# One kernel, two k halves on two DMA queues: new order of the first loads, masked S on GpSimd, k sketch split by row halves

## The chip, the cores and the metric

The kernel runs on one core of a Trainium2 chip. The metric is the device time of one execution in microseconds (us); of several executions the median is given. The engines are named as the profile names them: PE is TensorE (PEld its weight loads), DVE is VectorE, ACT is ScalarE, POOL is GpSimd, SP is SyncE. SP and ACT issue the DMAs.

## The reference, cut to what matters

A polynomial linear attention feeds one feed-forward layer. All inputs are float32; there are 4 batches and 4 heads, 1088 positions, head size 32, and sketches S1 and S2 of 8 rows each.

```python
def phi(x):
    a = np.einsum('rd,bhsd->bhsr', S1, x)
    b = np.einsum('rd,bhsd->bhsr', S2, x)
    return np.einsum('bhsi,bhsj->bhsij', a, b).reshape(*x.shape[:-1], r * r)
q_p, k_p = phi(q), phi(k)
kv = np.einsum('bhsf,bhsd->bhfd', k_p, v)
z = np.sum(k_p, axis=2)
attn = np.einsum('bhsf,bhfd->bhsd', q_p, kv) / (np.einsum('bhsf,bhf->bhs', q_p, z)[..., None] + 1e-06)
x = attn as 4352 tokens x 128
h = x @ w_in                    # 128 -> 2048
out = (h - np.tanh(h)) @ w_out  # 2048 -> 128
```

## The kernel before, in words

The attention is computed batch by batch, the feed-forward in ten groups of tokens (192 to 512 columns each). The first group of tokens (384 columns) needs only the first 12 of the 34 q blocks of batch 0, and a special path (`q_heads`) makes them early. Until that group's x is there, PE has little to do, and runs matmuls on zeros (`f` of 256 and `F` of 512 columns) to stay busy. From then on PE works through the matmuls of the feed-forward (`h` and `o`) with the attention of the other batches between them.

Every operation is added to a program with its inputs and outputs (`P.add`), under a name. The order on each engine is not worked out when the kernel is built: it is written out in `TABLE`, a list of tokens such as `66t:0` (operation 66, on TensorE, buffer choice 0). `plan` reads the table, and `sync` puts semaphore waits where an operation needs one of another engine. Each engine then works strictly in its order. An operation marked `lock` also waits for the last locked operation of the other engine of the pair DVE and POOL. Large loads carry an extra wait, so that at most `CAP` bytes are in flight.

The start of batch 0, which the change touches, goes so:

- Loads (line 465). `load_k(0)` asks for k of batch 0 in two halves by columns, `lk0.0` and `lk0.1`, 272 KB each, on SP's queue; `sin1`, S2's load (16 KB), is on SP's queue too. `sin0` is S1's load, on ACT's queue. SP's order is `lk0.0`, `lk0.1`, `sin1`, then q, then v.
- Masks. POOL builds an identity matrix (lines 434, 435); DVE reduces it to `mask4` (line 439), `mask2` (442) and `maskh` (445).
- k transposes (line 560) on DVE, four of them: `kT0.0.0` and `kT0.1.0` of the first half (288 and 256 elements in each partition), `kT0.0.1` and `kT0.1.1` of the second.
- S. `stt` (line 524, DVE) transposes S1 and S2, which came by `sin0` and `sin1`; `wab` (line 527) multiplies it by `mask2`.
- Sketch. `ksk0.0` and `ksk0.1` (line 580, PE) are 16 calls in all, 32 matmuls in the profile: a call for each of four column groups and two row halves, for either half of k. `kab0.0` and `kab0.1` (line 591, DVE) transpose the result into `abk`, row half by row half.
- Outer products (line 646): `w0.0` on POOL, `w0.1` on DVE, `w0.2` on POOL, one after the other by the lock. `kvmm0.0` to `kvmm0.2` (line 661, PE) multiply them with v.
- The first q blocks: `qsk0.0`, `abc0.0`, `m0.0`, `den0.0` (line 712), `rd0.0` (714), `aq0.0` (POOL, 715), `qph0.0` and `qph0.1` (DVE, 722), `qpTh0.0` and `qpTh0.1` (728). In the same stretch stand `kvh` (689), `kve` (690), and, for the other 22 blocks, `m0.3` (774), `den0.3` (777) and `rd0.3` (780). POOL also copies S for batch 1, `wqc1` (534).
- `num0.0` and `num0.1` (line 735, PE), then the copies `x0.0.0` and `x0.0.1` (line 359), then the first feed-forward matmul `h0.0` (line 920).

Of the kernel before, what the change touches and what calls it, by code (L numbers as in the profile page):

```python
# [31 lines left out]
38s 125t:0 117v:0 251a:1 232g 253a:2 254t:0 43s 233g 256t:1 126v:1 280t:0 39s 255a:3 281t 282t 127v 258t:2 257a:4 234g
260t:0 119v 40s 128t:0 259a:5 262t:1 14g 283t 41s 129a:1 264t:2 261a:6 235v 284t 130t 263a:7 266t:0 36s 285t 265a:8
286t 131v:0 37s 133v:3 268t:1 287t 267a:9 288t 270t:2 269a:10 242t:0 134v:4 243t 271a:11 272t:1 289t 274t:2 273a:12
120t:0 45s 158v:0 275a:13 46s 132v 159v 276t:1 102s 244t 121a 135v:0 245t 44s 122a 278t:2 136t:0 277a:14 103s 137t
246a 138t 247v 48s 160t:1 142v 139a:1 105s 279a:15 303t:0 290t 104s 140t 161v:0 304a:16 305t:1 291t 162v 100s 307t:0
141a:1 309t:2 306a:17 143t:0 168g:1 308a:18 99s 310a:19 311t:0 292t 313t:1 144v:0 312a:20 293t 47s 315t:2 294t 314a:21
295t 101s 317t:0 316a:22 296t 319t:1 318a:23 297t 145g:0 321t:2 163t:0 320a:24 298v:0 323t:0 322a:25 57g 325t:1 146v:0
299s 164a:0 327t:2 324a:26 165t 335t:0 147v:0 326a:27 98s 336t 329t:0 166v:1 328a:0 148v:0 331t:1 300s 337t 330a:28
167v 333t:2 149g:1 177v 338t 301s 332a:29 339t 340t 341t 334a:1 358t:0 302s 360t:1 362t:2 359a:2 178t:0 151g:2 361a:30  # L40
150v:1 363a:31 364t:0 342t 366t:1 343t 365a:3 179v:1 368t:2 344t 367a:4 345t 153g:0 370t:0 369a:32 346t 372t:1 371a:33
374t:2 347t 152v 373a:5 348t 376t:0 375a:6 378t:1 180g:1 349t 377a:7 350t 154v 351t 380t:2 379a:8 352t 382t:0 381a:9
384t:1 353v:1 155t:0 383a:10 181v:1 354s 385a:11 355s 390t:0 356s 386t:0 157v 156a 391t 392t 357s 388t:1 393t 387a:12
170v:2 413t:2 394t 389a:13 415t:0 414a:14 395t 417t:1 182v:1 396t 212v 416a:15 397t 183g:1 398t 419t:2 418a:16 421t:0
184g:1 399t 400t 420a:17 401t 193v:0 423t:1 402t 422a:18 403t 404t 194v 425t:2 424a:19 405t 169g:3 406t 427t:0 426a:20
407t 429t:1 428a:21 431t:2 408v:2 195t:0 430a:22 185v:0 409s 58g 186g:2 432a:23 433t:0 410s 435t:1 196v:1 437t:2
434a:24 411s 171t:2 197v 436a:25 172t 412s 203g:4 198t:0 438a:26 173t 199a:1 439t:0 200t 174v:0 441t:1 440a:27 445t:0
11g 201v:0 443t:2 187v 188g:0 446t 442a:0 468t:0 447t 444a:28 470t:1 202v 175t 469a:29 472t:2 448t 59g 176v:2 471a:1
204g:0 474t:0 213t:0 189v 473a:2 475a:30 476t:1 449t 214v:0 205g:1 478t:2 477a:31 480t:0 450t 479a:3 451t 482t:1
481a:4 452t 453t 454t 483a:32 215v:0 484t:0 486t:2 216v:0 488t:1 485a:33 190t:0 217v:0 487a:5 218v:0 489a:6 219g:1  # L50
490t:0 191v 492t:1 455t 491a:7 494t:2 456t 192v 221g:2 493a:8 496t:0 457t 495a:9 458t 220v:1 498t:1 459t 497a:10 460t
523t:2 223g:0 499a:11 222v 461t 462t 524a:12 526t:0 529t:1 463v:0 206t:0 527a:13 207t 525v 530a:14 464s 532t:2 528v
500t:0 465s 531v 501t 533a:15 224v 535t:0 466s 502t 538t:1 536a:16 503t 467s 534v 504t 539a:17 537v 541t:2 505t 544t:0
540v 542a:18 506t 547t:1 545a:19 507t 543v 508t 548a:20 550t:2 546v 509t 510t 551a:21 549v 553t:0 511t 556t:1 552v
554a:22 512t 559t:2 557a:23 513t 555v 514t 560a:24 562t:0 558v 515t 516t 563a:25 561v 565t:1 517t 568t:2 564v 566a:26
208t 518v:1 569a:27 598t:0 567v 519s 571t:0 570v 599a:0 601t:1 572t 520s 604t:2 602a:28 600v 573t 521s 574t 605a:29
607t:0 603v 575t 522s 576t 608a:1 606v 610t:1 577t 613t:2 609v 611a:2 578t 579t 209v:1 616t:0 614a:30 580t 612v 581t
617a:31 582t 615v 619t:1 583t 618v 622t:2 620a:3 584t 625t:0 623a:4 585t 621v 586t 626a:32 587t 624v 628t:1 210t 627v
631t:2 629a:33 588t 211v:3 634t:0 632a:5 225t:0 630v 635a:6 589v:2 633v 590s 636v 637t:1 591s 646t:0 227a 226v 640t:0
592s 643t:2 638a:7 647t 648t 593s 641a:8 669t:0 639v 670t 594s 644a:9 673t:1 642v 649t 674t 671a:5 595s 645v 677t:2  # L60
650t 596s 651t 652t 675a:6 672v 678t 597s 653t 654t 655t 656t 679a:7 681t:0 676v 682t 657t 658t 659t 683a:8 680v
685t:1 686t 660t 661t 687a:9 684v 689t:2 690t 662t 663t 691a:10 701t:1 688v 693t:0 694t 702t 703t 695a:11 692v 697t:1
704t 698t 664v:0 705t 728t:2 699a:12 706t 696v 729t 665s 707t 708t 666s 730a:13 709t 700v 710t 732t:0 733t 667s 711t
712t 734a:14 731v 668s 736t:1 737t 713t 714t 738a:0 740t:2 735v 741t 715t 716t 742a:15 717t 739v 718t 744t:0 745t
760t:0 743v 748t:1 746a:1 749t 761t 762t 719v:1 752t:2 750a:16 753t 763t 747v 720s 764t 765t 721s 754a:2 766t 751v
756t:0 757t 722s 767t 768t 783t:1 758a:3 755v 769t 723s 770t 771t 784t 724s 772t 786t:2 787t 785a:4 759v 773t 725s
774t 788a:5 789t:1 790t 775t 726s 792t:0 793t 791a:6 795t:2 776t 727s 796t 794a:7 798t:1 799t 777t 797a:8 807t:1
801t:0 808t 802t 778v:2 800a:9 809t 804t:2 805t 810t 811t 803a:10 812t 813t 814t 781s 815t 816t 806a:11 817t 818t 819t
820t 779a 821t 782s 822t 823t 824t 780a 825v:0 827a 826s 829a 828s
# [260 lines left out]
def bass_polysketch_attn__then__act_tanh_shrink_kernel(  # L330
# [177 lines left out]

    load_s(0, S1, "scalar")
    load_k(0)  # L510
# [8 lines left out]
    for b in range(1, B - 1):  # L519
# [3 lines left out]

    P.add(_v(64), lambda e, n: e.transpose(
        stt.ap.rearrange("p x d -> p (x d)"), sin.ap.rearrange("p x d -> p (x d)")),
        r=[sin], w=[stt], name="stt")
    P.add(_v(32), lambda e, n: e.tensor_tensor(
        out=wab.ap.rearrange("p (x e i) -> p x e i", e=2, x=2),
        in0=stt.ap.rearrange("p x (r i) -> p x r i", i=8)[:, :, 0:2, :],
        in1=mask2.ap[:, None, :, None].to_broadcast([128, 2, 2, 8]), op=ALU.mult),  # L530
        r=[stt, mask2], w=[wab], name="wab", lock=True)
    for i, (w, z) in enumerate(zip(wqc, wqs)):
        P.add(_g(8), lambda e, n, z=z: e.memset(z[:, 24:32], 0.0), w=[w], name=f"wqz{i}")
        P.add(_g(16), lambda e, n, w=w: e.tensor_copy(
            w.ap.rearrange("p (x i) -> p x i", i=8), stt.ap.rearrange("p x (r i) -> p x r i", i=8)[:, :, 0, :]),
            r=[stt], w=[w], name=f"wqc{i}", lock=True)
    P.add(_gt(64), lambda e, n: e.tensor_tensor(
        out=wqdc.ap.rearrange("p h (x i) -> p h x i", i=8),
        in0=stt.ap.rearrange("p x (r i) -> p x r i", i=8)[:, None, :, 0, :].to_broadcast([128, H, 2, 8]),
        in1=maskh.ap[:, :, None, None].to_broadcast([128, H, 2, 8]), op=ALU.mult),  # L540
        r=[stt, maskh], w=[wqdc], name="wqd", lock=True)
    P.add(_gt(128), lambda e, n: e.tensor_tensor(
        out=s2r.ap.rearrange("p (h d) -> p h d", h=H),
        in0=sin.ap[:, 1, None, :].to_broadcast([128, H, 32]),
        in1=mask4.ap[:, :, None].to_broadcast([128, H, 32]), op=ALU.mult),
        r=[sin, mask4], w=[s2r], name="s2r", lock=True)

# [291 lines left out]
    def q_front(b, s0, s1):  # L839
        abc = _Val(abc_p)  # L840
        q_sketch(b, s0, s1, abc)
        return abc, q_divide(b, s0, s1, abc)

    def attention():
        k_transposes(0)
        k_sketch(0)
        gram(0)
        for p in range(3):
# [190 lines left out]
```

## Time and profile before

| what | value |
|---|---|
| time, median of 3 runs | 104.55 us (104.22 to 104.70) |
| the profiled execution's own time | 104.33 us |
| its span | 102.2 us |
| busy: PE, DVE, ACT, POOL | 94.9, 79.1, 79.7, 35.6 us |
| first feed-forward matmul (line 920) | starts at 17.33 us |
| feed-forward groups, tanh on ACT (line 924) | 40.5 + 16.8 + 16.6 us busy |
| DMA | 11.37 MB, 111 GB/s over the span |

The span runs from the first to the last instruction that the profile shows; the 2.1 us by which the execution's own time is longer lie around it. Times of instructions count from the start of the span. An engine's busy time says how long its instructions ran; what an engine waited for stands behind an arrow. The chain of waits is followed back from the last instruction, at each step to what released it.

### The profile page before, as it was taken

The numbers are of one execution on the slowest core, as the hardware profiler recorded it, in microseconds if no ns is written. First come the engines' busy times: TensorE is split into PE (matmuls) and PEld (weight loads), VectorE is DVE, ScalarE is ACT, GpSimd is POOL, SyncE is SP. The second block draws the span as 40 slices with busy tenths as digits, with TensorE's granted clock in tenths as the row PEclk, the third lists the DMA queues.
The fourth block names the chain that finished last, engine by engine and source line by source line (L and its number), as shares of the span: only waits on it lengthen the run. The fifth ranks groups of instructions, "written<-read, shape, count | busy, mean of one in ns | idle before, by whom it ended". The sixth has DMA issues, their size and how long they took to land.

```text
span 102.2 us, 3037 instructions
## 1 busy us (share of the span) xinstructions
PE 94.9 (93%) x1252; PEld 48.3 (47%) x1261; DVE 79.1 (77%) x146; ACT 79.7 (78%) x157; POOL 35.6 (35%) x53
## 2 busy tenths in 40 slices
PE   5998979999999999999999999999999999999950
PEld 2243546466645455555535343444453444444740
DVE  2678699989848896976697788687898789999420
ACT  4001395997689996999899798999988999999930
POOL 4066829900053991299892970000000000000000
PEclk9999999999999999999999999999999999999999
DMA  2987998999988811303100003305000410601555
GB/s 49 293 272 186 339 275 237 278 313 335 302 251 274 189 20 23 47 7 61 17 0 6 0 0 57 52 0 91 12 0 15 74 21 0 103 0 22 79 77 75
DMA packets 25917, 11.37 MB, mean 111 GB/s; under 512 B 19120, under 2 KB 23600, under 8 KB 25904
## 3 DMA queue, kind: packets, MB, share of 16 engines
q1 hardware_dynamic: 24288, 10.98, 42.2%
q10 hardware_dynamic: 1616, 0.20, 1.3%
q8 instruction: 10, 0.16, 0.7%
q14 instruction: 3, 0.02, 0.1%
HBM read 8.95 MB, written 2.23 MB: 109 GB/s over the span
## 4 chain that ended last, share of the span: by engine, by line
PE 64%; DVE 12%; POOL 9%; ACT 4%; issue 3%; DMA 3%; SPq 1%; DVEq 0%
PE psb L941 23%; PE psb L920 22%; POOL qp L800 4%; POOL w L646 4%; PE psb L661 4%; PE psb L580 3%; DMA sin<-in_S_dram 3%; PE psb L816 3%; DVE th L929 2%; DVE ot L950 2%; PE psb L945 2%; PE psb L757 2%; ACT wi_f L924 2%; PE psb L735 2%; DVE qp L722 1%
## 5 line engine op out<-in xcount | busy, mean ns | idle before, releaser
L920 PE MATMUL psb<-xT,wi 128*128 128x512 bf16 (+3 forms) x152 | 46.2, 347 | 0.2 <-issue 0.2
L924 ACT ACTIVATE th<-psb 128x512 bf16<-128x512 f32 (+3 forms) x77 | 40.5, 594 | 3.1 <-PE psb L920 1.8
L941 PE MATMUL psb<-th,wo 128*128 128x512 bf16 (+3 forms) x89 | 26.2, 343 | 0.5 <-DVE ot L950 0.2
L920 PEld LDWEIGHTS psb<-xT,wi 128*128 128x128 bf16 x160 | 14.8, 97 | 22.9 <-ACT th L924 4.4
L800 POOL TENSOR_TENSOR qp<-ap,abc 128x768 f32<-128x768 f32 x11 | 16.4, 1513 | 3.8 <-DVE ap L782 3.4
L924 ACT ACTIVATE wi_f<-psb 128x512 bf16<-128x512 f32 (+3 forms) x31 | 16.8, 612 | 0.5 <-PE psb L920 0.3
L924 ACT ACTIVATE wo_f<-psb 128x512 bf16<-128x512 f32 (+2 forms) x28 | 16.6, 626 | 0.7 <-PE psb L661 0.4
L929 DVE TENSOR_TENSOR th<-psb,th 128x320 bf16<-128x320 f32 (+2 forms) x24 | 13.2, 562 | 2.4 <-ACT th L924 1.6
L646 POOL TENSOR_TENSOR w<-abk 128x768 f32<-128x768 f32 x7 | 10.6, 1516 | 9.4 <-DVE abk L591 8.4
L941 PEld LDWEIGHTS psb<-th,wo 128*128 128x128 bf16 x90 | 8.6, 99 | 5.7 <-issue 0.5
L805 DVE STREAM_TRANSPOSE qpT<-qp 128x768 f32<-128x768 f32 x11 | 10.4, 955 | 0.6 <-POOL qp L800 0.6
L941 PE MATMUL psb<-wo_f,wo 128*128 128x512 bf16 (+1 forms) x32 | 10.4, 362 | 0.4 <-DVE th L929 0.4
L941 PE MATMUL psb<-wi_f,wo 128*128 128x512 bf16 (+2 forms) x38 | 10.3, 344 | 0.1
L430 PE MATMUL psb<-zz 128*128 128x512 bf16 x24 | 8.0, 456 | 1.1 <-DVE zz L428 1.1
L950 DVE STREAM_TRANSPOSE ot<-psb 128x512 f32<-128x512 f32 (+3 forms) x10 | 6.3, 628 | 3.3 <-PE psb L941 2.1
L929 DVE TENSOR_TENSOR wi_f<-psb,wi_f 128x192 bf16<-128x192 f32 (+1 forms) x12 | 6.1, 510 | 1.6 <-ACT wi_f L924 0.9
L929 DVE TENSOR_TENSOR wo_f<-psb,wo_f 128x320 bf16<-128x320 f32 (+2 forms) x12 | 6.8, 576 | 0.4 <-ACT wo_f L924 0.2
L560 DVE STREAM_TRANSPOSE kT<-kL 128x576 f32<-128x576 f32 (+3 forms) x10 | 5.8, 610 | 1.3 <-DMA kL<-in_k_dram 1.3
L762 DVE STREAM_TRANSPOSE abc<-psb 128x1152 f32<-128x1152 f32 (+1 forms) x4 | 5.1, 1273 | 1.9 <-PE psb L757 1.9
L816 PE MATMUL psb<-qpT,kvb 32*32 32x288 f32 (+1 forms) x256 | 6.1, 392 | 0.0
L661 PE MATMUL psb<-w,vL 128*32 128x64 f32 x288 | 5.4, 221 | 0.1
L661 PEld LDWEIGHTS psb<-w,vL 128*32 128x32 f32 x288 | 4.4, 110 | 1.8 <-issue 1.3
(89 smaller groups left out, 98.0 us busy)
## 6 DMA issues: line engine op xcount, KB each, us to landing
vL<-in_v_dram SPq DMA_DIRECT2D x16, 144.0 KB, 4.1
kL<-in_k_dram SPq DMA_DIRECT2D x8, 272.0 KB, 4.5
qL<-in_q_dram SPq DMA_DIRECT2D x6, 272.0 KB, 4.3
wi_f<-in_moe_w_in_dram SPq DMA_DIRECT2D x4, 256.0 KB, 5.4
wo_f<-in_moe_w_out_dram SPq DMA_DIRECT2D x4, 256.0 KB, 4.3
out_dram<-ot SPq DMA_DIRECT2D x14, 64.0 KB, 2.0
out_dram<-ot SPq DMA_DIRECT2D x8, 48.0 KB, 3.2
qL<-in_q_dram SPq DMA_DIRECT2D x2, 176.0 KB, 3.3
```

What stands on the lines that cost most here:

```text
L430: "F": lambda e, n: e.matmul(bank(3), zz.ap[:, 0:128], zz.ap[:, None, 128:384].to_broadcast([128, 2, 256]), start=True, stop=True)}, zop)
L560: P.add(_v(nb * 32 * (r1 - r0)), lambda e, n, e_=e_, nb=nb, r0=r0, r1=r1: e.transpose(kTv[b][r0].ap.rearrange("p (j u t r) -> p r j u t", ...
L646: P.add({**_v(768), **_gt(768)}, lambda e, n: e.tensor_tensor(out=wv.ap.rearrange("p (x i j) -> p x i j", i=8, j=8), in0=abh(0)[:, :, :, N ...
L661: i = e.matmul(pv[b].ap[h * 32:(h + 1) * 32, 0:64], vL[b][:, h, blk * 32:(blk + 1) * 32], wvs[b, p].ap[:, (bi * 4 + h) * 64:(bi * 4 + h + ...
L800: P.add({**_v(cn * 256), **_gt(cn * 256)}, lambda e, n, qp=qp, c0=c0, cn=cn: e.tensor_tensor(out=qp.ap[:, 0:cn * 256].rearrange("p (x i j) ...
L805: P.add(_v(cn * 256), lambda e, n, qp=qp, o0=o0, cn=cn: e.transpose(qt.ap[:, o0 * 256:(o0 + cn) * 256], qp.ap[:, 0:cn * 256]), r=[qp], w=[ ...
L816: i = e.matmul(psa4[h * 32:(h + 1) * 32, g, 0:nb * 32], kvb.ap[g * 32:(g + 1) * 32, x, h * 32:(h + 1) * 32], qq[g * 32:(g + 1) * 32, 0:nb, ...
L920: P.add(_mm(n_), lambda e, n, jb=jb, hv=hv: e.matmul(hv.ap[:, jb % m * 512:jb % m * 512 + n_], wi[jb // 4].ap[:, (jb % 4) * 128:(jb % 4 + ...
L924: act = P.add(_a(n_ * m), lambda e, n, hv=hv, th=th: e.activation(out=th.ap.rearrange("p (u x) -> p u x", u=m)[:, :, 0:n_], in_=hv.ap.rear ...
L929: P.add(_vp(gc * m), lambda e, n, hv=hv, th=th: e.tensor_tensor(out=th.ap.rearrange("p (u x) -> p u x", u=m)[:, :, 0:gc], in0=hv.ap.rearra ...
L941: fn = lambda e, n, x=x, st=st, sp_=sp_: e.matmul(ov.ap[:, 0:n_], wo[x // 4].ap[:, x % 4, :], ths[x][0].ap[:, ths[x][1] * 512:ths[x][1] * ...
L950: P.add(_vp(n_), lambda e, n: e.transpose(ot.ap[:, 0:n_], ov.ap[:, 0:n_]), r=[ov], w=[ot], name=f"ot{gi}")
```

## The change

The code changes in four places.

1. `load_k(0)` now comes ahead of `load_s(0, S1, "scalar")`, and the second half of k, `lk0.1`, is issued on ACT's queue. On ACT's queue the order is `lk0.1`, then `sin0`; on SP's it is `lk0.0`, then `sin1`, then q and v.
2. The block that makes the weights out of S moves into a function `s_weights()`, called after the k transposes, and `stt` must follow `kT0.0.1`.
3. `wab` may run on POOL, and the new table puts it there.
4. `ksk0.1` is split into two operations by row half, `ksk0.1` (first row half) and `ksk0.2` (second), so that `kab0.0` waits only for the first of them.

```diff
     def load_k(b):
         src = k[b].rearrange("h (t c) d -> (h t) (c d)", c=NC)
         for r in range(2):
-            load(kL[b][:, r * 544:(r + 1) * 544], src[:, r * 544:(r + 1) * 544], [kvals[b][r]], 128 * 544 * 4, 128, name=f"lk{b}.{r}")
+            load(kL[b][:, r * 544:(r + 1) * 544], src[:, r * 544:(r + 1) * 544], [kvals[b][r]], 128 * 544 * 4, 128, eng="scalar" if (b, r) == (0, 1) else "sync", occ=650.0 if (b, r) == (0, 1) else 415.0, name=f"lk{b}.{r}")
             if b == 0 and r == 0:
                 load_s(1, S2, "sync")
...
+    load_k(0)
     load_s(0, S1, "scalar")
-    load_k(0)
     load_q(0, 0)
...
+    def s_weights():
+        P.add(_v(64), lambda e, n: e.transpose(
+            stt.ap.rearrange("p x d -> p (x d)"), sin.ap.rearrange("p x d -> p (x d)")),
+            r=[sin], w=[stt], name="stt", after=[x for x in P.ops if x.name == "kT0.0.1"])
+        P.add({**_v(32), **_gt(32)}, lambda e, n: e.tensor_tensor(
+            out=wab.ap.rearrange("p (x e i) -> p x e i", e=2, x=2),
...
-        def sk(e, n, m0=0, ms=1):
+        def sk(e, n, m0=0, ms=1, rhs=(0, 1)):
             for g in range(4):
-                for rh in range(2):
+                for rh in rhs:
...
         if b == 0:
-            for r in range(2):
-                P.add(_pe(317, 245.0), lambda e, n, r=r: sk(e, n, r, 2), r=[kTv[b][r], wab], w=pk, mode="64x32", name=f"ksk{b}.{r}")
+            P.add(_pe(317, 245.0), lambda e, n: sk(e, n, 0, 2), r=[kTv[b][0], wab], w=pk, mode="64x32", name=f"ksk{b}.0")
+            for rh in range(2):
+                P.add(_pe(159, 245.0), lambda e, n, rh=rh: sk(e, n, 1, 2, (rh,)), r=[kTv[b][1], wab], w=[pk[rh]], mode="64x32", name=f"ksk{b}.{1 + rh}")
```

The table is written anew. Put into names, its orders differ from those of before in these places up to the first feed-forward matmul:

- DVE: `mask2` stood between `mask4` and `kT0.0.0`, and now stands between `kT0.1.0` and `kT0.0.1`; `wab` is gone; `den0.0` and `kvh` change places, and so do `kve` and `rd0.3`; `x0.0.0` is gone (it is on ACT, ahead of `x0.0.1`).
- POOL: `wab` stands right behind the identity matrix, ahead of `wqd`; four small fills and copies (`qpad0`, `qpad1`, `wqc0`, `wqdz`) stand later than they did.
- PE: one more `f` ahead of `ksk0.0`; of the fillers between the sketch and `num0.0` some are moved, and the `f` between `kvmm0.1` and `kvmm0.2` is gone. The numbers of `f` and `F` in the whole program change by one `f` less.
- SP: `lk0.1` is gone; `lq0.1.1` and `lq0.0.0` change places.

Behind the first feed-forward matmul the new table swaps neighbours in a few dozen places on PE (an `o` matmul and an `h` matmul, mostly), gives some banks and buffers other numbers, moves `x0.3.0` from ACT to DVE, `w1.2` ahead of `kT2.0.0` and `wo0` ahead of `qp0.6`, and changes the order in which SP asks for the later q and v pieces.

More of the change, by code (lines that the diff above doesn't have):

```diff
@@ L32 @@
[L32 to L36, printed above, removed]
@@ new lines @@
+8g 77v:1 7g F F F 85t:0 35s 75v 78g:2 111t:0 86v:0 79t:1 112v:1 80t 87g:0 81t 9g 88v:0 113g:1 34s 229a 82v 89v:0 59g
+90g:0 114v:1 108a:0 28s F F F F 109t 230a 91v:0 237t:0 95v:1 49s 231a 238t 115v:1 83v 240t:1 31s 232a 92v:0 116g:1
+239a 96v:1 F 241t 117g:2 32s 110v:0 93t:2 242a 97t:1 33s 94a 124v:0 98a f F F 249t:0 125v 233g 251t:1 42s 253t:2
+250a:0 38s 126t:0 118v:0 119g:0 252a:1 254a:2 255t:0 43s 281t:0 127v:1 257t:1 256a:3 282t 40s 283t 128v 259t:2 234g
+258a:4 261t:0 120v 41s 129t:0 260a:5 263t:1 61g 235g 284t 39s 130a:1 265t:2 262a:6 285t 131t 14g 264a:7 286t 236v
@@ new lines @@
+449t 473t:2 472a:28 205g:0 475t:0 190v 214t:0 474a:29 476a:3 477t:1 479t:2 215v:0 206g:1 450t 478a:30 451t 481t:0
+480a:31 483t:1 452t 482a:4 453t 485t:2 454t 484a:5 216v:0 455t 487t:0 486a:32 217v:0 489t:1 191t:0 488a:33 218v:0
+490a:6 219v:0 220g:1 491t:0 192v 493t:1 495t:2 492a:7 456t 457t 193v 222g:2 494a:8 497t:0 458t 496a:9 459t 221v:1
+499t:1 460t 498a:10 524t:2 461t 224g:0 500a:11 223v 462t 463t 525a:12 527t:0 530t:1 464v:0 207t:0 528a:13 208t 526v
+531a:14 465s 533t:2 529v 501t:0 466s 532v 502t 534a:15 225v 536t:0 467s 503t 539t:1 537a:16 504t 468s 535v 505t
@@ new lines @@
+540a:17 538v 542t:2 506t 545t:0 541v 543a:18 507t 548t:1 546a:19 508t 544v 509t 549a:20 551t:2 547v 510t 511t 552a:21
+550v 554t:0 512t 557t:1 553v 555a:22 513t 560t:2 558a:23 514t 556v 515t 561a:24 563t:0 559v 516t 517t 564a:25 562v
+566t:1 518t 569t:2 565v 567a:26 209t 519v:1 570a:27 599t:0 568v 520s 572t:0 571v 600a:0 602t:1 573t 521s 605t:2 603a:1
+601v 574t 522s 575t 606a:2 608t:0 604v 576t 523s 577t 609a:28 607v 611t:1 578t 614t:2 610v 612a:29 579t 580t 210v:1
+617t:0 615a:3 581t 613v 582t 618a:30 583t 616v 620t:1 584t 619v 623t:2 621a:31 585t 626t:0 624a:4 586t 622v 587t
@@ new lines @@
+627a:5 588t 625v 629t:1 211t 628v 632t:2 630a:32 589t 212v:3 635t:0 633a:33 226t:0 631v 636a:6 634v 590v:2 638t:1 637v
+591s 647t:0 228a 227v 641t:0 592s 644t:2 639a:7 648t 593s 649t 642a:8 670t:0 640v 671t 594s 645a:9 674t:1 643v 650t
+595s 675t 672a:5 646v 678t:2 651t 596s 652t 679t 676a:6 597s 673v 653t 654t 655t 656t 598s 657t 680a:7 682t:0 677v
+683t 658t 659t 660t 684a:8 681v 686t:1 687t 661t 662t 688a:9 685v 690t:2 691t 663t 664t 692a:10 694t:0 689v 702t:1
+703t 695t 704t 693v 698t:1 696a:11 705t 699t 665v:0 706t 707t 700a:12 729t:2 697v 730t 666s 708t 709t 667s 731a:13
@@ L70 @@
+817t 807a:11 818t 819t 820t 821t 783s 822t 780a 823t 824t 825t 781a 826v:0 828a 827s 830a 829s
 """
@@ L522, in bass_polysketch_attn__then__act_tanh_shrink_kernel @@
         load_v(b)
[L524 to L546, printed above, removed]
     xvals = []
@@ L563, in k_transposes @@
                     r=kvals[b][r0:r1], w=kTv[b][r0:r1], name=f"kT{b}.{e_}.{r0}")
+    def s_weights():
[4 more added lines that the diff above has]
+            out=wab.ap.rearrange("p (x e i) -> p x e i", e=2, x=2),
+            in0=stt.ap.rearrange("p x (r i) -> p x r i", i=8)[:, :, 0:2, :],
+            in1=mask2.ap[:, None, :, None].to_broadcast([128, 2, 2, 8]), op=ALU.mult),
+            r=[stt, mask2], w=[wab], name="wab", lock=True)
+        for i, (w, z) in enumerate(zip(wqc, wqs)):
+            P.add(_g(8), lambda e, n, z=z: e.memset(z[:, 24:32], 0.0), w=[w], name=f"wqz{i}")
+            P.add(_g(16), lambda e, n, w=w: e.tensor_copy(
+                w.ap.rearrange("p (x i) -> p x i", i=8), stt.ap.rearrange("p x (r i) -> p x r i", i=8)[:, :, 0, :]),
+                r=[stt], w=[w], name=f"wqc{i}", lock=True)
+        P.add(_gt(64), lambda e, n: e.tensor_tensor(
+            out=wqdc.ap.rearrange("p h (x i) -> p h x i", i=8),
+            in0=stt.ap.rearrange("p x (r i) -> p x r i", i=8)[:, None, :, 0, :].to_broadcast([128, H, 2, 8]),
+            in1=maskh.ap[:, :, None, None].to_broadcast([128, H, 2, 8]), op=ALU.mult),
+            r=[stt, maskh], w=[wqdc], name="wqd", lock=True)
+        P.add(_gt(128), lambda e, n: e.tensor_tensor(
+            out=s2r.ap.rearrange("p (h d) -> p h d", h=H),
+            in0=sin.ap[:, 1, None, :].to_broadcast([128, H, 32]),
+            in1=mask4.ap[:, :, None].to_broadcast([128, H, 32]), op=ALU.mult),
+            r=[sin, mask4], w=[s2r], name="s2r", lock=True)
     def q_transpose(b, i):
@@ L845, in attention @@
         k_transposes(0)
+        s_weights()
         k_sketch(0)
```

60 lines of the change are left out of this document (22 added, 38 removed).

## The prediction

> **What bounds the kernel now.** I read the page first: its slices for the engine that is never idle, and the chain for what ended last.
>
> ```profile
> PE   5998979999999999999999999999999999999950
> ...
> PE 64%; DVE 12%; POOL 9%; ACT 4%; issue 3%; DMA 3%; SPq 1%; DVEq 0%
> ```
>
> PE carries the chain. The busy time by stretches says from when on that is work and not filler (columns: stretch, its length, then PE, PEld, DVE, ACT, POOL busy, the granted clock, the DMA share and GB/s):
>
> ```profile
> 2.00:2.50 0.50, 0.50 (x3) 0.23 (x2) 0.19 (x1) 0.50 (x1) 0.00 (x0) 1.00 0.57 157
> 2.50:3.00 0.50, 0.50 (x3) 0.18 (x2) 0.00 (x0) 0.19 (x1) 0.00 (x0) 1.00 1.01 364
> ...
> 17.30:25.00 7.70, 7.70 (x140) 4.24 (x140) 7.28 (x14) 6.33 (x16) 3.04 (x5) 1.00 0.96 301
> 25.00:40.00 15.00, 15.00 (x286) 8.14 (x297) 12.23 (x19) 13.37 (x38) 7.65 (x7) 1.00 0.67 188
> ```
>
> From 17.3 us, where the first feed-forward matmul starts, PE has no idle time to 40 us, at full clock, and little behind it. So the end moves with the start of that matmul, one to one, and the question is what the change does to the 17.3 us before it. There the chain in order of time runs through S's landing (4.64), `stt` (4.69), `wab`, the sketch, `abk`, `w0.0`, `w0.1`, the q sketch, and then (start, duration, what):
>
> ```profile
> 10.53 0.88 PE psb L661 x48
> 11.41 0.22 PE psb L429
> 11.62 0.52 PE psb L661 x24
> 12.16 0.25 DVE kvh L689
> 12.41 0.16 DVE den L712
> 12.60 0.24 DVE rd L714
> 12.90 0.36 POOL ap L715
> ```
>
> Next the timeline of DVE and POOL, since the chain names S's landing as the first wait and DVE's queue might be as late:
>
> ```profile
> 1.71 0.28 DVE L439 TENSOR_REDUCE mask<-ident 128x4 f32<-128x128 f32 x1 [0.65 <-POOL ident L435]
> 1.91 0.28 DVE L442 TENSOR_REDUCE mask<-ident 128x2 f32<-128x128 f32 x1
> 3.52 1.25 DVE L560 STREAM_TRANSPOSE kT<-kL 128x288 f32<-128x288 f32 x3 [1.33 <-DMA kL<-in_k_dram]
> 4.69 0.21 DVE L524 STREAM_TRANSPOSE stt<-sin 128x64 f32<-128x64 f32 x1
> 4.94 0.19 DVE L527 TENSOR_TENSOR wab<-stt,mask 128x32 f32<-128x32 f32 x1
> 5.05 0.44 DVE L560 STREAM_TRANSPOSE kT<-kL 128x256 f32<-128x256 f32 x1
> ...
> 5.74 0.30 POOL L537 TENSOR_TENSOR wqd<-stt,maskh 128x64 f32<-128x64 f32 x1 [4.06 <-DVE maskh L445]
> ...
> 11.80 0.59 POOL L774 TENSOR_TENSOR m<-abc 128x192 f32<-128x192 f32 x1
> ```
>
> It is: DVE ran three k transposes back to back from 3.52 to 4.77, and `stt` follows without a gap (an instruction may start some 0.08 before the recorded end of the one ahead). S's landing and DVE's queue end together. The idle 1.33 us stand before the first transpose, which waits for k's first half. Asked for at 0.73 and 1.19, k's halves took (us from the start of the issue to the landing)
>
> ```profile
> DMA to landing us min/median/max: 2.8/2.9/3.1
> ```
>
> so they landed at about 3.50 and 4.27; the two S loads, asked for at 0.75 and 1.66 and 2.9 and 3.0 us on the way, at 3.69 and 4.64.
>
> **Part one, the loads.** S2 is issued 0.47 us earlier (at about 1.18) and S1 behind k's half on ACT's queue, at 1.15 to 1.4; at 2.95 each they land at 4.15 to 4.35. That removes S from the chain, but not DVE's queue. k's second half is asked for at 0.75, beside the first, and the price is what this does to the first. From 2.50 on the 16 DMA engines were full (share 1.01), with 0.57 in the half microsecond before. If the second queue fills that gap, 0.43 x 0.5 = 0.21 us are won for the pair, which then ends at 4.27 - 0.21 = 4.06. The first half lands between 3.50 (undisturbed) and that, or at 4.27 if nothing is won. The trace of before has no two large loads side by side. I take the middle of 3.50 and 4.06, 3.8: ACT's issue may start a little later (its one issue took 0.63, SP's of k 0.40), and the second half's bytes must then get in between. Cost on the first transpose: **+0.30**, ends 0 and +0.77.
>
> The Trainium skill, DMA: Bandwidth & Descriptors, Queues, rings and completion order, says that each DMA engine takes turns between the queues with work for it, packet by packet; Issuing engines are not separate DMA queues, there, says that issuing on several engines saves only time on the sequencer. By these the halves would land close together and late, and the first rival below would hold. The trace agrees as far as it goes: S1, on ACT's queue, landed at 3.69, before k's second half.
>
> **Part two, `mask2`.** It ran at 1.91 in DVE's idle time, at no cost; now it stands between two transposes. `mask4` and `mask2` start 0.20 apart, so it costs **+0.20** as long as k's second half is there by the time it ends (0.97 behind the first landing, which the pair's end fulfils); were that half later still, the delay would be that half's. So `stt` starts 1.19 + 0.20 = 1.39 behind the first landing: 5.19 in place of 4.69. S is there by then, with 0.8 to spare.
>
> **Part three, `wab` on POOL.** POOL's masked products took 0.30 for 64 elements and 0.41 for 128 (`s2r`); by the slope 32 elements take 0.24, against 0.19 on DVE. The hand-over from DVE to POOL took 0.08 (`maskh` done 5.65, `wqd` 5.74), from DVE to DVE 0.03. POOL is idle then. The first sketch starts 0.10 later behind `stt`. In return `kT0.1.1` starts 0.19 earlier, but the 16 matmuls of `ksk0.0` take 0.37 before `ksk0.1` can start, and both waits ended together in the run before, so it is the later one that counts: **+0.10** (ends 0.05 and 0.15). What POOL has queued behind `wab` (`wqd`, `qpad0`, `s2r`, `wqz2`, `idb`, `qpad1`, `wqc0`, together 1.2) is done 0.4 before `abk` lets `w0.0` go.
>
> **Part four, the sketch by row halves.** The 16 matmuls of `ksk0.1` started, by their rows in the trace, in two bunches of 8, 0.18 apart, each bunch through within 0.05: the row halves run side by side. `kab0.0` is released by the last of the first row half, some **-0.03** earlier; if the halves should run in turn, up to -0.19. `kab0.1` follows 0.41 behind `kab0.0` and hides the second half.
>
> **Part five, the order around `kvh`.** `w0.2` was done at 11.27, but `f` (the 0.22 at 11.41) stood before `kvmm0.2`; without it that starts at about 11.40, and `kvh` 0.2 earlier. `den0.0` waited behind `kvh`, though `m0.0` was done at 11.61; ahead of it, it runs in DVE's idle 0.54, and `rd0.0` starts 0.17 behind `kvh` in place of 0.43. That would be -0.46 for `aq0.0` (12.90 to 12.44). POOL's queue stops it: `m0.3` ran to 12.39 and `wqc1` stands behind it, so `aq0.0` starts at 12.49: **-0.41**. From `qph0.0` to `num0.0` the same work follows (`kve` and `rd0.3` only change places), so all of it counts.
>
> **Nothing:** `x0.0.0` on ACT (0.32 to 0.36) lies in the 0.71 in which ACT waited for `num0.1`; with that cover gone it would cost 0.32. q, v and `w_in` are asked for 0.46 earlier, but no wait of the chain is for them. The extra `f` lies ahead of `ksk0.0`, where PE now waits longer. The neighbours swapped behind 17.3 us are the same matmuls on a full PE: 0, give or take 0.3.
>
> **Sum:** +0.30 + 0.20 + 0.10 - 0.03 - 0.41 = +0.16. On the profiled execution, span 102.2 and own time 104.33, that gives 102.4 and 104.5; that execution is 0.22 below the median 104.55, to which I add the same: **104.7**. A measurement of this kernel can tell about 0.5% (0.52 us) from no change.
>
> **Rival 1, the halves share the engines to the end.** The first half lands with the second at 4.27, nothing is won: +0.77 + 0.20 + 0.10 - 0.03 - 0.41 = +0.63, 105.2, slower. For it: the full share from 2.50 on. Against it: the idle share ahead of that, and k's first half has a head start. It decides from a landing of 4.16 on (+0.66 - 0.14 = 0.52). By the rule of the page named above, this is the case.
>
> **Rival 2, S's landing was the bound, as the chain has it.** Then `stt` would follow S at 4.35, 0.34 earlier, and with +0.10 - 0.03 - 0.41 the sum is -0.68: 103.9, faster. Against it: `kT0.0.1` ended at 4.77, and the changed code puts `stt` behind it. It needs k to land earlier, which nothing here does; only an undisturbed first half (-0.14) together with better packing where PE still had idle time (by stretches 0.46 from 40 to 60, 0.70 from 60 to 80) comes near.
>
> **Rival 3, the second queue leaves the first half alone**: it lands at 3.50 as before, because ACT's DMA comes to the engines only when the first half is nearly through. Then +0.20 + 0.10 - 0.03 - 0.41 = -0.14, 104.4; with the row halves in turn (-0.16 more) 104.2. Both are within 0.5%. For it: S1's load, asked for at 0.75 on ACT's queue, landed behind k's first half. Against it: S1 is another shape, and S2 took as long on SP.
>
> **How the numbers follow.** Forecast (a first landing of 3.6 to 4.1): 0.47, and rival 3: 0.15, together 0.62, within 0.5%. Rival 1: 0.25. Rival 2 and its neighbours: 0.13. The range takes rival 3's 104.2 as its lower end; at the top rival 1's 105.2 with 0.1 of what lies behind 17.3: 105.3. Outside lie rival 2 and the worst of rival 1.
>
> **What the changed profile would show.** The first `kT` at 3.8 and not 3.52; the wait for k's first half longer than 1.33; `stt` near 5.2, released by DVE and not by S; `wab` on POOL in 0.24; `kab0.0` 1.6 behind `stt`; `aq0.0` at 12.90 + 0.57 - 0.41 = 13.06; the first feed-forward matmul at 17.5. It is wrong if the first `kT` starts before 3.5 or after 4.2, if `stt` waits for S, or if PE's busy time behind 17.3 us has new gaps.

## The result, and the profile after

| | before | after |
|---|---|---|
| time, median of 20 runs each | 104.64 us (104.22 to 105.68) | 105.53 us (104.64 to 106.30) |
| ratio | | 1.006, 95% interval 1.0036 to 1.0084 |
| the profiled execution's own time | 104.33 | 105.75 |
| its span | 102.2 | 103.6 |
| first feed-forward matmul | 17.33 | 18.25 |

The changed kernel is slower, by 0.6%: 0.63 us by the ratio (its interval is 0.38 to 0.88 us), 0.89 by the medians, 0.70 by the means of the 20 runs. The interval lies on both sides of the 0.5% from which a difference counts here. The two profiled executions differ by more, 1.42. One run of the changed kernel, 106.30, over 1.5% above its fastest, is left out of the ratio.

The page of the changed kernel, slices of PE and the chain by engine:

```profile
PE   5959998999989999999999999999999999999960
...
PE 67%; POOL 12%; DVE 11%; DMA 4%; issue 3%; DVEq 0%
```

PE still carries the chain. SP's queue is gone from it, but DMA has grown from 3% to 4%. The chain in order of time says what that DMA is (start, duration, what):

```profile
0.73 3.70 DMA kL<-in_k_dram
...
5.36 0.48 DVE kT L536
5.83 0.02 issue
5.86 0.26 DVE stt L542
6.11 0.07 issue
6.18 0.25 POOL wab L545
6.43 0.04 issue
6.48 0.97 PE psb L581 x32
...
8.40 1.52 POOL w L648
...
13.03 0.59 POOL m L776
13.62 0.14 POOL wq L552
13.76 0.31 POOL ap L717
...
16.15 1.69 PE psb L737 x8
```

S's landing is off the chain, and k's first half stands in its place: asked for at 0.73 as before, landed at 4.44 (before 3.50). The DMA issues of the first 7 us, each with the KB and the us to landing:

```profile
kL<-in_k_dram SPq DMA_DIRECT2D x1, 272.0 KB, 3.7
kL<-in_k_dram ACTq DMA_DIRECT2D x1, 272.0 KB, 3.9
...
sin<-in_S_dram ACTq DMA_DIRECT2D x1, 16.0 KB, 3.9
sin<-in_S_dram SPq DMA_DIRECT2D x1, 16.0 KB, 4.0
```

All four loads take 0.8 to 1.0 us longer than the 2.8 to 3.1 of before. k's second half, asked for 0.45 earlier, lands at 4.62 (before 4.27), S1 at 5.04 and S2 at 5.22. By stretches (columns as for the kernel before):

```profile
2.00:2.50 0.50, 0.50 (x2) 0.15 (x1) 0.00 (x0) 0.50 (x1) 0.00 (x0) 1.00 0.68 244
2.50:3.00 0.50, 0.50 (x2) 0.15 (x1) 0.00 (x0) 0.50 (x1) 0.00 (x0) 1.00 1.00 387
...
18.25:25.00 6.75, 6.75 (x114) 3.99 (x120) 5.61 (x10) 6.02 (x15) 2.92 (x6) 1.00 0.91 294
25.00:40.00 15.00, 14.66 (x265) 7.51 (x261) 12.21 (x20) 11.78 (x34) 7.34 (x6) 1.00 0.66 191
```

The second queue did move more in the gap before 2.50 (244 GB/s in place of 157), and PE has no idle time again from the first feed-forward matmul on; but between 25 and 40 us it now lacks 0.34, which before were none. The timeline of DVE, with POOL's `wab`:

```profile
4.46 0.81 DVE L536 STREAM_TRANSPOSE kT<-kL 128x288 f32<-128x288 f32 x2 [2.55 <-DMA kL<-in_k_dram]
5.19 0.24 DVE L442 TENSOR_REDUCE mask<-ident 128x2 f32<-128x128 f32 x1
5.36 0.47 DVE L536 STREAM_TRANSPOSE kT<-kL 128x288 f32<-128x288 f32 x1
5.86 0.24 DVE L542 STREAM_TRANSPOSE stt<-sin 128x64 f32<-128x64 f32 x1
6.03 0.40 DVE L536 STREAM_TRANSPOSE kT<-kL 128x256 f32<-128x256 f32 x1
...
6.18 0.24 POOL L545 TENSOR_TENSOR wab<-stt,mask 128x32 f32<-128x32 f32 x1 [4.59 <-DVE stt L542]
```

Up to the first feed-forward matmul, the delay against before grows and shrinks in these steps (starts in the two traces):

| step | before | after | delay | its part |
|---|---|---|---|---|
| first `kT` | 3.52 | 4.46 | 0.94 | 0.94 loads |
| third `kT` (`kT0.0.1`) | 4.29 | 5.36 | 1.07 | 0.13 `mask2` |
| `stt` | 4.69 | 5.86 | 1.17 | 0.10 `stt` starts behind the end of `kT0.0.1` |
| `kab0.0` | 6.24 | 7.47 | 1.23 | 0.06 `wab` on POOL and the row halves |
| `aq0.0` | 12.90 | 13.71 | 0.81 | -0.42 order round `kvh` |
| `num0.0` | 15.35 | 16.15 | 0.80 | |
| first feed-forward matmul | 17.33 | 18.25 | 0.92 | 0.12 `num0` pair, 1.69 in place of 1.57 |

At the first matmul of the q sketch of the second batch (32 matmuls) the delay is 0.80 (28.59 and 29.39). Then, in the changed kernel, this sketch stops half way; chain in order of time:

```profile
29.46 0.64 PE psb L759 x15
30.10 0.28 issue
30.38 0.72 PE psb L759 x17
```

In the kernel before, the same sketch ran without a stop (the chain counts 28 of its 32 matmuls here):

```profile
28.66 0.87 PE psb L757 x28
```

That is the rest: 1.64 in place of 0.87, +0.77 (0.15 of it came back by the end of the span). "issue" names no producer: the profile shows nothing that PE waited for.

### The profile page after: what moved, and what is told of

It reads as the page before. It is cut to its first block, busy times and chain, and to the rows that moved or that the text cites. A ratio compares the mean times of both kernels' runs of the same rounds, so it can differ in the third digit from the quotient of the medians.

```text
span 103.6 us, 3040 instructions
## 1 busy us (share of the span) xinstructions
PE 96.8 (93%) x1260; PEld 48.4 (47%) x1260; DVE 79.5 (77%) x145; ACT 79.1 (76%) x157; POOL 35.7 (34%) x54
## 4 chain that ended last, share of the span: by engine, by line
PE 67%; POOL 12%; DVE 11%; DMA 4%; issue 3%; DVEq 0%
PE psb L923 24%; PE psb L944 24%; POOL w L648 6%; POOL qp L802 4%; PE psb L818 4%; DMA kL<-in_k_dram 4%; PE psb L581 3%; PE psb L663 3%; PE psb L948 2%; PE psb L759 2%; PE psb L737 2%; DVE ot L953 2%; DVE qT L573 1%; DVE kT L536 1%; DVE qp L724 1%
## 5 line engine op out<-in xcount | busy, mean ns | idle before, releaser
L923 PE MATMUL psb<-xT,wi 128*128 128x512 bf16 (+3 forms) x160 | 48.8, 349 | 0.2 <-DVE th L932 0.2
L944 PE MATMUL psb<-wo_f,wo 128*128 128x512 bf16 (+1 forms) x32 | 10.9, 363 | 0.0
L573 DVE STREAM_TRANSPOSE qT<-qL 128x1088 f32<-128x1088 f32 (+2 forms) x5 | 5.2, 1055 | 0.0
```

The source lines that it names most:

```text
L923: P.add(_mm(n_), lambda e, n, jb=jb, hv=hv: e.matmul(hv.ap[:, jb % m * 512:jb % m * 512 + n_], wi[jb // 4].ap[:, (jb % 4) * 128:(jb % 4 + ...
L944: fn = lambda e, n, x=x, st=st, sp_=sp_: e.matmul(ov.ap[:, 0:n_], wo[x // 4].ap[:, x % 4, :], ths[x][0].ap[:, ths[x][1] * 512:ths[x][1] * ...
```

## Experiments

My theory from these two profiles, A: k's first half lands later, because the halves share the DMA engines, and the rest of the change costs nothing. Its rival, B: the late part of the new table, where PE stalled, costs the time. A third question came with the runs: why the times differ less than the profiles. Ratios are against the kernel before on the same chip. The profiled executions of e5, e8 and e10 were longer than most of their kernel's, so only their steps up to the first feed-forward matmul, and in e10 what PE waited for, are read from them.

**e1, the change with its four loads as before.**

```diff
-  load(kL[b] ..., eng="scalar" if (b, r) == (0, 1) else "sync", ...)
+  load(kL[b] ..., name=f"lk{b}.{r}")      # table: lk0.0, sin0, lk0.1, sin1 as before
```

> The changed kernel with the four loads as before: both k halves on SyncE's queue, S1 first on ScalarE's, S2 third on SyncE's; all the rest (wab on GpSimd, the row halves, mask2 between the transposes, the new table) stays. Theory A, the late landing of k's first half is the cause: the first k transpose starts at 3.5 us as before and not at 4.46, stt at 3.50 + 1.42 = 4.92, the first feed-forward matmul at 17.33 + 0.13 + 0.10 + 0.06 - 0.42 + 0.12 = 17.3, and the time is that of the kernel before, within 0.3 us. Theory B, the loss is made by the new order behind the first feed-forward matmul (PE stood in the q sketch of the second batch at 29.7 to 30.4): the time stays 0.5 to 0.9 us above the kernel before, with that stall in the profile, though the first feed-forward matmul is at 17.3.

Measured: 104.87 us, ratio 0.9995 (0.9962 to 1.0029). With the loads of before the loss does not show: the interval ends below that of the first measurement of the change (1.0036 to 1.0084), though it overlaps with that of e4 (1.0011 to 1.0073). `stt` ran at 4.92 as expected. But the first feed-forward matmul started at 17.74 and not at 17.3, because the sketch was held up elsewhere. Chain of e1:

```profile
1.51 4.27 PE psb L430 x10
5.78 1.16 PE psb L581 x32
```

The ten zero matmuls (`F`) ahead of the sketch took 0.43 each to the end, and the sketch after them 1.16, where 0.97 stands in the changed kernel. The table shows no loss of its own: from the first feed-forward matmul to the end of the span it took 84.58 us here, the shortest of all profiles, and 84.87 before. B isn't borne out.

**e2, the loads alone.**

```diff
-  load(kL[b] ..., name=f"lk{b}.{r}")
+  load(kL[b] ..., eng="scalar" if (b, r) == (0, 1) else "sync", name=f"lk{b}.{r}")
```

> The kernel before with only the loads of the change: k's second half first on ScalarE's queue, S1 behind it, S2 second on SyncE's. Theory A: the first k transpose starts at about 4.45, stt 1.19 later, all of the 0.94 us reaches the first feed-forward matmul (18.3), and the time is 0.9 us above the kernel before (105.5). Theory B: the loads cost little, 104.6 to 104.9.

Measured: 104.94 us, ratio 1.0013 (0.9984 to 1.0042): a miss. A had 105.5, B 104.6 to 104.9. The chain has A's mechanism,

```profile
0.73 3.58 DMA kL<-in_k_dram
4.32 0.02 issue
4.34 0.38 DVE kT L560
```

with the second half at 4.50 and 0.77 of delay at the first feed-forward matmul (18.11). But the ratio gives +0.13%, and +0.42% at the end of its interval. The first feed-forward matmul comes only 0.14 ahead of that of the changed kernel; the profiles part behind it: to the end of the span it took 84.67 here, 85.38 and 85.01 (e4) in the changed kernel, where the q sketch stopped, in whole or in part. The kernel before, too, may not run in every execution as early as in its first profile; e3, e7 and e12 follow that up.

**e3, the order round `kvh` alone.**

```diff
-79t 86g:0 f 80t 9g 112g:1 34s 228a 81v 87v:0       (f, kvmm0.2 ... kvh, den0.0)
+79t 86g:0 80t 9g 112g:1 34s 228a 87v:0 81v         (kvmm0.2 ... den0.0, kvh; kve behind rd0.3)
```

> The kernel before with only the order around kvh: den0.0 ahead of kvh, rd0.3 ahead of kve, no f between kvmm0.1 and kvmm0.2. By the prediction's term -0.41 (measured in the changed kernel as -0.42 between w0.0 and aq0.0): the ap product of the first q blocks at 12.49 in place of 12.90, the first feed-forward matmul at 16.9, the time 0.4 us below the kernel before. If PE was not bound from 17.3 us on, nothing of it reaches the end.

Measured: 104.52 us, ratio 0.9972 (0.9937 to 1.0007): the lowest of all, and not clear of 1. The term itself is there: `aq0.0` came 5.31 behind `w0.0`, before 5.73, so -0.42. This execution lost it again at both ends: S2 landed at 4.91 (before 4.64), the `F` ran to 5.56 and `w0.0` started 0.30 late; and the q sketch stopped, with the table of before at that place:

```profile
28.50 0.64 PE psb L757 x14
29.14 0.32 issue
29.46 0.73 PE psb L757 x18
```

So the stop at 29 us needs neither the new table nor the new loads. What makes it stays open.

**e4, the changed kernel once more, no edit.**

> The changed kernel once more, for a second profile. If the landing at 4.44 and the stall of PE at 29.7 belong to the kernel and not to one execution, both are there again: first k transpose at 4.3 to 4.6, first feed-forward matmul at 18.1 to 18.4, a gap of over 0.3 us in the q sketch of the second batch. If the stall is of that one execution, the distance of the two kernels at the end is that at the first feed-forward matmul, 0.8 to 0.9 us.

Measured: 105.24 us, ratio 1.0042 (1.0011 to 1.0073). The front repeats within 0.03: first `kT` at 4.49, `stt` 5.88, `w0.0` 8.43, feed-forward 18.28. The q sketch lost only 0.22, with no gap of over 0.3; the own time was 105.42.

**e5, the changed kernel with `mask2` early and `stt` free of its demand.**

```diff
-... 4v 19s ... 50v:0 51v 20s 5v 52v 22s 54v ...    (mask4 ... kT kT mask2 kT0.0.1 stt)
+... 4v 5v 19s ... 50v:0 51v 20s 52v 22s 54v ...    (mask4 mask2 ... kT kT kT0.0.1 stt)
-  name="stt", after=[x for x in P.ops if x.name == "kT0.0.1"])
+  name="stt")
```

> The changed kernel with mask2 back behind mask4 (before k lands) and without the demand that stt follow kT0.0.1; the order on VectorE is still kT0.0.0, kT0.1.0, kT0.0.1, stt. Theory A, the landing of k's first half and then VectorE's queue are the bound: the first k transpose stays at 4.45 to 4.5, but stt comes 1.19 behind it, not 1.40 to 1.42, so at 5.65; sketch, w0.0 and the first feed-forward matmul come 0.2 us earlier than in the changed kernel (18.05), the time is 0.2 below it. Rival, S's landing (4.8 to 5.2 in the changed kernel) holds stt: then nothing moves.

Measured: 105.05 us, ratio 1.0041 (1.0012 to 1.0071). In the timeline of e5

```profile
4.44 1.16 DVE L536 STREAM_TRANSPOSE kT<-kL 128x288 f32<-128x288 f32 x3 [2.33 <-DMA kL<-in_k_dram]
5.53 0.20 DVE L542 STREAM_TRANSPOSE stt<-sin 128x64 f32<-128x64 f32 x1
```

`stt` stands 1.09 behind the first transpose, in the changed kernel 1.40. Of the 0.31, `mask2` and the demand explain 0.13 + 0.10 by the table above; the kernel before took 1.17, so the last 0.08 belong to neither. S2's landing, at 5.21, did not hold `stt`. The feed-forward started at 17.88, 0.37 before that of the changed kernel. The time shows no such gain: its interval lies on e4's.

**e6, a staggered load: S1, then k's second half on ACT, S2 on SP behind the first half.** On the kernel before.

```diff
 SP:  lk0.0, lk0.1, sin1, q ...   ->   lk0.0, sin1, q ...
 ACT: sin0                        ->   sin0, lk0.1
```

> The kernel before with S1 first on ScalarE's queue and k's second half behind it there (asked for at about 1.4 in place of 0.75), S2 second on SyncE's. If the two halves share the DMA engines from the moment that both are asked for, a second half that comes 0.6 us later leaves the first half a head start: first k transpose at 3.6 to 4.0, between 3.5 (both on SyncE's queue) and 4.34 to 4.49 (both at once). If a second queue as such delays the first, it is at 4.3 or later. The time: the kernel before plus that delay where PE's fillers do not hide it.

Measured: 106.9 us, ratio 1.0218 (1.0178 to 1.0259): slower, by 1.8 to 2.6%. With 0.69 of a head start the first half landed at 3.57, as if alone. But the second half was then late (chain of e6, and below it the granted clock by slices of 2.6 us from its page):

```profile
1.42 4.71 DMA kL<-in_k_dram
6.13 0.02 issue
6.15 0.04 DVE kT L560
...
8.43 1.71 PE psb L430 x4
...
PEclk9995999999999999999999999999999999999999
```

It took 4.71, beside S2 (4.6) and the q loads that SP had asked for meanwhile; which of them held it up is not separated. The late start then cost again. PE stood idle from 4.92 to 7.04 us, and the trace's records of the granted clock stand at half from 7.54 to 10.96: `F` took 0.43 each at 8.43, where they took 0.22 before, and the feed-forward started at 20.13.

**e7, the kernel before with 9 `F` ahead of the sketch in place of 10.**

```diff
-F F F 66t:0        (F F F ksk0.0)
+F F 66t:0
```

> The kernel before with nine F ahead of the sketch in place of ten. Theory C: in the profile of before the zero matmuls started 0.427 us apart and from 4.1 us on 0.21 to 0.28 apart; in two other profiles with the old loads they stayed 0.427 apart to the end, and the sketch began at 5.5 to 5.7, behind the fillers, not behind wab at 5.19. So in part of its executions the kernel before waits for its own fillers, and loses up to 0.4 us, which hid part of what the later landing costs. With nine, the last filler starts at 4.5 and is through at 4.94 even at 0.427 each: the sketch starts at 5.2 in every execution, and the median falls by 0.1 to 0.3 us. If the fillers do not matter, no change.

Measured: 104.85 us, ratio 0.9999 (0.9968 to 1.003). The median did not fall. The sketch could start at 5.17, but took 1.30 (1.03 before), and `w0.0` came at 7.42. The last section has the reason: in this execution the full clock came only at 6.47. That moment differs from execution to execution, so one profile does not say whether the missing `F` moved it.

**e8, e3 and e7 together.**

> The kernel before with the order around kvh of the change (den0.0 ahead of kvh, rd0.3 ahead of kve, no f between kvmm0.1 and kvmm0.2) and nine F ahead of the sketch. By both terms 0.41 + 0.1 to 0.3 us below the kernel before: 104.0 to 104.2 in the median, first feed-forward matmul at 16.9. A PE stall of 0.5 to 0.8 us in the q sketch of the second batch, as in two of six profiles so far, can still hit single executions.

Measured: 104.98 us, ratio 1.0014 (0.9983 to 1.0044). In its profile S2 landed at 5.17 and held `stt` (5.20):

```profile
1.66 3.51 DMA sin<-in_S_dram
5.17 0.02 issue
5.20 0.26 DVE stt L524
```

PE then ran its `F` 0.43 us apart up to 9 us, and the feed-forward came at 18.83; `aq0.0` stood 6.44 behind `w0.0`, so that the gain of the new order did not show here. Expected were 104.0 to 104.2: a miss.

**e9, S2 behind S1 on ACT's queue, k untouched, on the kernel before.**

```diff
-                load_s(1, S2, "sync")
+                load_s(1, S2, "scalar")
```

> The kernel before with S2 behind S1 on ScalarE's queue, both k halves on SyncE's. In five profiles with S2 third on SyncE's queue it landed at 4.43 to 5.17 us, and where it was late, stt waited for it (4.93 and 5.20 in place of 4.69). On the other queue, asked for at 1.4, it should land at about 4.35 whatever k does, with the first k transpose still at 3.5: stt at 4.7 in every execution, and the median 0.1 to 0.3 us below the kernel before. If two queues share the engines to k's cost, k's second half lands later than 4.3 and stt is at 4.9 or later.

Measured: 104.98 us, ratio 1.0014 (0.9984 to 1.0044). The halves landed at 3.55 and 4.26, untouched; S2, asked for at 1.41, came at 4.90, later than the 4.35 expected. Asking earlier did not make it land earlier. Expected was a gain of 0.1 to 0.3: a miss.

**e10, fewer bytes in flight late: 0.8 MB in place of 1.45 from the 23rd large load on.**

```diff
-  left = CAP - o.dma[0]
+  left = (CAP if len(loads) < 22 else LATE) - o.dma[0]
```

> The kernel before with less in flight from the 23rd large load on (k's second half of batch 2, asked for at 18 us): 0.8 in place of 1.45 million bytes. Theory D: PE's stall at 28 to 30 us is a wait for its own instructions; in the four profiles that have it the third 16 KB packet of the instruction queue started at PE's weight load number 914 to 917 or took 2.2 us, and in those without at 742 to 890; the loads of batches 2 and 3 stand before it. With less in flight the packet starts by number 850 in this profile, the q sketch of the second batch has no gap, and the upper part of the times (over 105.2, in 11 of the first 35 runs of the kernel before) thins out. Rival: the loads become late and PE waits for q or v: slower.

Measured: 107.19 us median, 104.5 to 108.73. Eight of the twelve runs took 106.2 us or more; the ratio 1.0026 (0.9974 to 1.0078) rests on the other four and says little. In the profiled execution the theory's remedy exchanged one wait for another, as the rival had it: PE now waits for q (chain of e10, and below it the granted clock by slices from its page).

```profile
25.07 3.66 DMA qL<-in_q_dram
28.73 0.02 issue
28.76 1.31 DVE qT L573
...
PEclk9999999999996799999999999999999999999996
```

PE waited 1.9 us, and from 32.56 to 35.97 the granted clock stood at half. But e11 has the same limit, and eleven of its twelve runs took 104.2 to 105.4: what made so many runs of e10 long stays open. (The packet numbers in the expectation count PE's matmuls together with its weight loads.)

**e11, the kernel before with S2 on ACT (e9), the order round `kvh` (e3) and the late limit (e10).**

> The kernel before with S2 behind S1 on ScalarE's queue, the order around kvh of the change, and less in flight from the 23rd large load on. If the terms add: 0.41 from the order, 0.1 to 0.3 from S, 0.2 on average from the stall: 103.8 to 104.0 in the median.

Measured: 104.69 us, ratio 0.9992 (0.9965 to 1.002). S2 landed at 5.46, `w0.0` came at 8.00; `aq0.0` again 5.31 behind it (-0.42); no stop at 29 us. Expected were 103.8 to 104.0: a miss. In this profile the gain went into S2's landing.

**e12, the kernel before once more, no edit.**

> The kernel before once more, for a second profile. If the first profile (w0.0 at 7.17, own time 104.33 with a median of 104.64) was one of its good executions, w0.0 comes later here, at 7.3 to 7.9 as in the other profiles with the old loads, because PE's zero matmuls ran 0.427 us apart for longer or S2 landed later. If 7.17 is there again, the 0.9 us between the two kernels' profiles at the first feed-forward matmul is typical.

Measured: 104.60 us, ratio 0.9986 (0.996 to 1.0011). S2 landed at 4.47 and `w0.0` started at 7.19, 0.02 from the first profile: the late start that I expected here didn't show. v's fourth part landed at 10.66, which put 0.23 on the feed-forward start (17.56), and up to the end of the q sketch another 0.33 was lost. No version was clearly faster than the kernel before.

## Why the prediction was right in its direction and short in its size

Forecast was +0.16 us, no change that can be told, with a lean to slower. Measured: +0.63 by the ratio, which happens to be the sum of rival 1. On the 104.55 from which the forecast was made that is 105.2, inside the range; the median 105.53 is above its end. That it is inside is in part luck: the first landing came later than the worst case that the prediction had allowed for, two further costs were not in its sum, and by the first two profiles the front alone lost 0.92.

- **Part one failed: +0.30 was forecast, 0.94 measured** (0.97, 0.92 and 0.82 in e4, e5 and e2; 3.46 to 3.59 is where the first transpose starts in every run with both k halves on SP's queue). That is beyond its worse end, 0.77. The step that failed is "0.43 x 0.5 = 0.21 us are won for the pair, which then ends at 4.27 - 0.21 = 4.06", with the first half ahead of that: the pair ended at 4.62, and the first half 0.18 ahead of it. The packets in the trace show why. By 3.0 us 159 of the pair's 256 large packets had started (before 129), so the bulk was indeed early (150 in e2 and 171 in e5, but only 134 in e4; 129 to 141 in the profiles with the old loads). But 91 were of the first half and 68 of the second, where before the first 128 were all of the first. And a load has landed with its last packet: in the changed kernel 124 of the first half's 128 had ended by 3.52, the last at 3.98, and the second half's last at 4.16; before, the last ones ended at 3.12 and 3.93. From the last packet to the landing it took 0.34 to 0.46 in all four cases. I reasoned on the mean rate, and the landing goes by the tail.
- **Rival 1's mechanism held, its size did not.** The halves shared the engines to the end: 91 and 68 packets at 3.0 us, and landings 0.17 or 0.18 apart in all four profiles. The Trainium skill, DMA: Bandwidth & Descriptors, Queues, rings and completion order, says that each DMA engine takes turns packet by packet between the queues. The trace agrees with that by the same two numbers. Rival 1 had the pair end at 4.27 as before. Why its last packet came 0.23 later than that of one after the other, no run here separates: S's 256 packets and the q loads were moving too.
- **`mask2`: +0.20 forecast, 0.13 measured.** Right in kind. **`stt` behind `kT0.0.1`**: not in my sum. I had counted the 0.40 between the starts of before, where `stt` began 0.08 ahead of the recorded end; with the demand it starts 0.03 behind that end, +0.10. e5 takes both away, and `stt` moves up by 0.31.
- **`wab` and the row halves: +0.07 forecast, 0.06 measured**, `wab` 0.24 as forecast, `kab0.0` 1.61 behind `stt` (forecast 1.6): 0.12 more up to the sketch, 0.06 less from there to `kab0.0`.
- **Order round `kvh`: -0.41 forecast, -0.42 measured** between `w0.0` and `aq0.0` in the changed kernel, and the same in e1, e3, e4, e5 and e11; not in e8, where PE, still at half clock, came later. `aq0.0` starts behind `wqc1` on POOL's queue, as worked out (13.62 and 13.76 in the chain above).
- **`num0` pair: +0.12, unforeseen**, in all four profiles with the new table round it (after, e1, e4, e5), in none with the old. `num0.1` got another bank, whose last reader, the copy of a `kvb0` result, ended at 16.86, and its first matmul started at 16.92. That it was the bank is argued from these two times, and weakly: this matmul started 0.18 behind the one ahead of it, near the usual 0.16, and 0.10 was lost between it and the next (0.26). No run changed the bank alone. The pair in the kernel before (chain):

```profile
15.35 1.57 PE psb L735 x8
```

- **Gaps behind 17.3: named as a way to be wrong, and seen**, but not as a cost that only the change has (e3 has the stop too). Apart from them the end did move with the first feed-forward matmul, as the prediction had it. From there to the end of the span it took 84.58 to 84.87 in the seven profiles without a stop (before, e1, e2, e6, e7, e9, e11), 85.01 and 85.03 in two with a part of one (e4, e12), 85.38 and 85.70 in two with a whole one (the changed kernel, e3).

With the first landing as it was, my other steps give 0.94 + 0.20 + 0.10 - 0.03 - 0.41 = 0.80 for the feed-forward start; 0.92 was measured. **Why is the time only 0.6% up?** Each kernel has two profiles of its front (17.33, and 17.56 in e12; 18.25, and 18.28 in e4), and their means differ by 0.82. That lies inside the interval of the ratio, 0.38 to 0.88 us, and a little above that of e4, 0.12 to 0.76. So noise may be all there is to it. My other answer is that the kernel before often runs later than in its first profile. There `w0.0` started so (chain):

```profile
7.17 1.52 POOL w L646
```

It came at 7.19 in e12, which speaks against that answer, and at 7.42 to 7.97 in e3, e7, e8 and e10, which differ from it in the front by one `F` at most. The mean of the six is 7.48; in the changed kernel it is 8.42 (8.40, 8.43). That leaves 0.94 and not 1.24 for the front, and with -0.42 + 0.12 a delay of 0.64. This is an estimate from few executions, and two of them (e8, e10) were long ones; without these the mean is 7.31 and the delay 0.81. What made the late ones late are two things that the delayed sketch of the changed kernel hides: S2's landing (4.43 to 5.17) and the moment at which PE gets its full clock (last section). That they are the reason for the smaller difference is argued, not shown: by the same reckoning e2 should lose 0.46 (0.77 - 0.31), its interval ends at 0.44, and e7 and e9, which attacked the two things, gained nothing.

Open, too, is the share of the stop in the q sketch: it came whole in 1 of 3 profiles with the new loads and in part in another, and whole in 1 and in part in another of the 8 with other loads (those set aside above, e5, e8 and e10, are not counted). By so few no difference in frequency can be told.

## What to carry to other kernels

Two large loads asked for at once on two queues did not arrive like one after the other, only sooner: both arrived with the tail of the pair (4.44 and 4.62, where one behind the other on one queue gave 3.50 and 4.27). Where the first piece feeds the chain, let the second follow it on the same queue: asked for 0.69 later on the other queue (e6), it left the first alone, but landed itself at 6.13. And judge a landing by the last packet, not by the mean rate. A step that the chain names as the bound (here S's landing) can be taken away for nothing, when another queue ends at the same time.

## What the runs showed of the hardware that I had not expected

- Zero matmuls of 512 columns started 0.427 us apart at first and 0.216 apart later. The rows of the stretches print a granted clock of 1.00 for both, and that misleads: the first record of the clock in a trace, at 1.00, begins at 4.21 before, 4.30 in e12, 4.96 in the changed kernel, 4.75 in e4, 3.78 in e5 and 4.13 in e6, and in each of these six the spacing changes there; the rows print 1.00 ahead of it for want of a record. In e1, e2, e7 and e8 it begins at 6.94, 6.64, 6.47 and 10.38, behind the start of the sketch, whose 32 matmuls then took 1.12 to 1.22 from the first start to the last end, where they took 0.95 or 0.96 at full clock (before, e12, the changed kernel, e3). So the moment differs from execution to execution by more than the change costs. The Trainium skill, TensorE: Matmul & The Clock Gate, Part 1, gives 426.7 ns cold and 215.7 warm for 512 columns, with some 3.4 us of activity to warm up. The two intervals agree with the trace; from the first zero matmul at 1.12 it took 2.7 us in e5 and 5.8 in e1, where PE ran without a gap. And the clock can go back: after PE had waited 2.1 us (e6) and 1.9 us (e10), it stood at half for 3.41 us each.
- PE can stop where the profile shows nothing that it waits for. In the changed kernel an instruction packet of 16 KB (the page counts 10 of them, queue q8) started at 28.12, before at 25.82, amid the loads of the later batches, and PE stopped at 30.10. That PE ran out of instructions is an inference from this order in time. Counted by PE's weight loads, that packet started behind number 454 in the changed kernel and 440 and 453 in e4 and e12, which stopped in part; in the seven profiles without a stop behind number 364 to 437; in e3 behind 404, but there it took 2.17 us, elsewhere 0.88 to 1.12. e10, which thinned the loads, moved the wait elsewhere and did not test it.
- Loads of 16 KB were as slow as those of 272 KB (k's first half 2.7 to 3.7): S2 took 2.8 to 4.1 us, and 4.6 in e6; a second half of k asked for 0.69 behind the first, on the other queue, took 4.71.
